# Two tiles of v loaded in five transfers each: 112 rows, then two sets of eight rows

## The chip, the core and the metric

The kernel runs on one core of one Trainium2 chip. It is written in Bass, with the Tile framework for buffers and semaphores; the order of the work on each engine is the order of the program (`manual_schedule`). A core has a tensor engine (PE; its weight loads stand in the profile as PEld), a vector engine (DVE), a scalar engine (ACT), a general engine (POOL), a sequencer for transfers (SP), and 16 DMA engines that all queues share. The metric is the time of one execution on the device in microseconds. Before the change the median of three runs is 256.0 us (255.96 to 256.0).

## The reference

Two stages in a row. The first is a cross-covariance attention over channels, with q, k and v of shape 4 x 6400 x 256 in float32:

```
qn = q / (norm(q over the 6400 rows) + 1e-6);  kn likewise
a  = softmax(kn^T @ qn / tau)            # 256 x 256 for each of the 4 batches
x  = v @ a                               # 4 x 6400 x 256
```

The second is a mixture of eight rank-16 adapters on the 25600 rows of x: `logits = x @ w_gate`, the two largest of eight are chosen for each row and weighted by their softmax, and `out = x + sum over the chosen e of w_e * (x @ A_e) @ B_e`.

## The kernel before

A batch's 6400 rows lie on the 128 partitions as 128 x 50: partition p holds rows 50p to 50p + 49. One of the 50 is a chunk (128 rows of 256 channels). All loads of q, k and v are issued by POOL, and they turn float32 into bf16 on the way. A chunk is 1 KB of float32 for each partition, and 512 bytes in the tile.

The q and k of a batch come in five tiles of 10 chunks. The v of a batch comes in three tiles of 18, 16 and 16 chunks (`VP`), into a ring of three buffers (`VB`), and each tile of 18 takes one row of 18 KB from each partition's part of DRAM. Tile (b, s) is tile s of batch b. For the first batch each v tile is loaded in two transfers; for batches 1 and 2 each is one transfer of 128 rows; the very last tile has three.

Phase one works on batch 0 alone: for each chunk two matmuls add to the 256 x 256 product of k and q (`gram`, L217), ACT or DVE squares it (`square`, L207 and L209), and matmuls with ones sum the squares (`norm`, L228). A chain of small steps (`chain0` to `chain6`) turns this into the attention matrix. Then come 100 slots, 25 for each batch. A slot takes two chunks of v: four transposes on PE (L366), a copy out of PSUM, the product with the gate and the adapters (L472), and a slot or two later the product with the attention matrix (L488), the adapters' second product (L508) and a copy to a row of `ys` (L512). Five slots make a group; its output is one store of 1280 KB. The gram of the next batch is dealt into the same slots (`GRAM`), so that PE always has both.

The loads stand in one list, sorted by the slot at which each is needed; `load_more` walks down it, as far as buffers are free, at the start of every slot. So the loads go to POOL's queue in one fixed order. A buffer is free when its last reader is done; POOL then waits for that reader, and everything behind on POOL's queue waits with it. POOL does nothing else after the first 12 us. Stores of finished groups are held back (`send`, `DEFER`) and issued from ACT; the last ones go out from SP in smaller parts (`LAST`).

Completion of a transfer is counted by a semaphore that each of the 16 DMA engines raises by one when its share has landed; a waiting engine waits for all 16. The loads take eight such semaphores in turn, and the trace shows POOL waiting for the load eight before the one it is about to issue: the load that is issued at 68.87 us takes the semaphore of the load that landed at 68.34 us, the next, at 71.31 us, that of 70.76 us.

The change touches `load_more` (L151 is the load of a v tile) and adds a function beside it.

Of the kernel before, what the change touches and what calls it, by code (L numbers as in the profile page):

```python
# [16 lines left out]
def kernel(  # L17
# [16 lines left out]
    nc = tc.nc  # L34
    B, N, C = q.shape
    P = 128
# [13 lines left out]
    VP = [18, 16, 16]  # L50
    FIRST = 4
    DEFER = 7

    GRAM = {1: (0, 20), 2: (24, 45), 3: (49, 67)}
    assert B == 4 and NC == 50
# [3 lines left out]
    v_v = v.rearrange("b (p c) d -> b p c d", p=P)  # L59
# [24 lines left out]
    for b, (first, last) in GRAM.items():  # L84
        n = last - first + 1
        for c in range(NC):
            s = first + c * n // NC
# [28 lines left out]
    def piece(kind, c):  # L116

        if kind == "qk":
            return divmod(c, PC)
        s = 0  # L120
        while c >= VP[s]:
            c -= VP[s]
            s += 1
        return s, c

    def used(kind, b, c, n):
        left[kind][where[kind, b, piece(kind, c)[0]]] -= n

    def load_more(limit=1000):

        while limit and at_load[0] < len(loads):
            _, kind, b, s, o, parts = loads[at_load[0]]
            if (kind, b, s) not in where:
                n = len(left[kind])
                if n >= bufs[kind] and left[kind][n - bufs[kind]]:
                    return
                where[kind, b, s] = n
                left[kind].append(PC if kind == "qk" else VP[s])
                if kind == "qk":
                    t = qk_pool.tile([P, 2, PC, C], BF16, tag="qk", name="qk")  # L140
                else:
                    t = v_pool.tile([P, max(VP), C], BF16, tag="v", name="vt")
                tiles[kind][b, s] = t
            t = tiles[kind][b, s]
            c0 = s * PC if kind == "qk" else sum(VP[:s])
            for m in parts:
                if kind == "qk":
                    nc.gpsimd.dma_start(t[:, 0, o:o + m, :], q_v[b, :, c0 + o:c0 + o + m, :])  # L148
                    nc.gpsimd.dma_start(t[:, 1, o:o + m, :], k_v[b, :, c0 + o:c0 + o + m, :])
                else:  # L150
                    nc.gpsimd.dma_start(t[:, o:o + m, :], v_v[b, :, c0 + o:c0 + o + m, :])  # L151
                o += m
            at_load[0] += 1
            limit -= 1
# [11 lines left out]
    nc.sync.dma_start(bst, moe_B.rearrange("e r d -> (e r) d"))  # L166
    nc.sync.dma_start(ast, moe_A.rearrange("e (p cc) r -> p e (cc r)", p=P))
    load_more(3)
    ones_bf = const.tile([P, P], BF16)
    nc.vector.memset(ones_bf, 1.0)  # L170
# [4 lines left out]
    for c in range(0, FIRST, 2):  # L175
        t = tiles["qk"][0, 0]
        nc.vector.tensor_copy(t[:, 0, c:c + 2, :], stage[:, 0, c:c + 2, :])
        nc.scalar.copy(t[:, 1, c:c + 2, :], stage[:, 1, c:c + 2, :])
    load_more(1)
    ident = const.tile([P, P], BF16)  # L180
    make_identity(nc, ident)
    ident_f = const.tile([P, P], FP32)
    make_identity(nc, ident_f)
    load_more(3)

    wg_sb = const.tile([P, CC, E], BF16)
# [335 lines left out]
    def send(keep):  # L522


        eng = nc.scalar
        while len(unsent) > keep:
            gr = unsent.pop(0)
            c0, n = 2 * (gr["f"] - gr["b"] * NPAIR), 2 * gr["n"]
            eng.dma_start(out_v[gr["b"], :, c0:c0 + n, :], gr["ys"][:, 0:n, :])
# [43 lines left out]
    while nz < NPT or zq is not None or dq is not None:  # L573
# [26 lines left out]
        dq, zq = zq, u  # L600
        send(max(0, min(DEFER, DEFER - (slot - GRAM[B - 1][1]) // 4)))
        if behind:
# [53 lines left out]
```

## Time and profile before

The profiled execution took 255.87 us, of which the page's span is 254.1 us; 1.8 us lie around it. The median of the three runs, 256.0 us, is 0.1 us above it.

| what | value |
|---|---|
| median of 3 runs | 256.0 us |
| profiled execution, its span | 255.87 us, 254.1 us |
| PE busy | 220.4 us (87%) |
| ACT busy | 176.1 us (69%) |
| DVE busy | 152.7 us (60%) |
| POOL busy | 33.0 us (13%) |
| mean granted TensorE clock | 0.966 |
| HBM read, written | 78.91 MB, 26.21 MB: 414 GB/s over the span |

A row of the page's table of groups is: line, engine, operation, what it writes and reads, count, busy time and mean length. The page's second part cuts the span in 40 slices; its row DMA gives in tenths how busy the 16 DMA engines were together. The third part lists the queues: q0 is POOL's loads, q10 is ACT's stores, q1 is SP's transfers, q8 and q14 carry the engines' instructions. The sixth part lists transfers by issuing line, with the median time from issue to landing. The chain of work that ended last is followed back from the last instruction, and each step stands for what released the next one.

### The profile page before, as it was taken

The page shows a single profiled execution, that of the slowest core. Times are in us where ns is not written, and L with a number is a line of the kernel's source. Part 1 is how long each engine was busy: PE and PEld are TensorE (multiplying, and loading weights), DVE is VectorE, ACT ScalarE, POOL GpSimd, SP SyncE. Part 2 cuts the span into 40 slices and gives each one's busy share as a digit, 9 for nine tenths or more (in the row PEclk, how much of TensorE's full clock was granted, in tenths as well). Part 3 has the DMA queues.
Part 4 walks back from the last instruction along what each step waited for, and adds up shares of the span by engine and source line. Part 5 has one row for each costly group of instructions (what it writes and reads, how often), then busy time and mean ns, then how long its engine had stood idle before and what let it go on. Part 6 is the DMA issues. An engine that isn't in the chain of part 4 may idle for free.

```text
span 254.1 us, 7393 instructions
## 1 busy us (share of the span) xinstructions
PE 220.4 (87%) x3106; PEld 190.2 (75%) x3106; DVE 152.7 (60%) x577; ACT 176.1 (69%) x290; POOL 33.0 (13%) x67
## 2 busy tenths in 40 slices
PE   0787793985999999999999989999999899999950
PEld 0444461775899978989999778989997799998940
DVE  1322235453567678685776876767587876778720
ACT  3434344776488698887878778888867777887860
POOL 8131221112112100110110202000000200000000
PEclk9999998696899999999999999999999999999997
DMA  7999999999999999999999999999999999999995
GB/s 213 223 217 215 212 216 214 213 216 216 210 214 215 223 207 215 218 212 214 215 220 211 214 270 259 236 296 281 255 291 292 389 326 362 414 420 426 423 412 220
DMA packets 13745, 66.80 MB, mean 263 GB/s; under 512 B 2576, under 2 KB 2704, under 8 KB 10384
## 3 DMA queue, kind: packets, MB, share of 16 engines
q0 software_dynamic: 8496, 38.80, 74.8%
q10 hardware_dynamic: 2592, 23.59, 22.4%
q1 hardware_dynamic: 2624, 3.94, 4.7%
q8 instruction: 24, 0.39, 0.6%
q14 instruction: 9, 0.07, 0.1%
HBM read 78.91 MB, written 26.21 MB: 414 GB/s over the span
## 4 chain that ended last, share of the span: by engine, by line
PE 58%; DMA 25%; DVE 7%; ACT 3%; issue 2%; POOL 1%; DVEq 0%; POOLq 0%; ACTq 0%
DMA qk<-in_k_dram 20%; PE y_ps L488 15%; PE acc L217 11%; PE zg L472 7%; PE y_ps L508 7%; PE vT_ps L366 6%; DMA out_dram<-ys 5%; PE zg L496 4%; PE nrm L234 3%; PE vT_ps L387 3%; ACT sq L207 2%; DVE gz L476 2%; ACT ys L512 1%; DVE lm L422 1%; DVE e L418 1%
## 5 line engine op out<-in xcount | busy, mean ns | idle before, releaser
L207 ACT ACTIVATE sq<-qk 128x1024 bf16<-128x1024 bf16 x87 | 89.6, 1054 | 22.1 <-DMA qk<-in_k_dram 16.8
L217 PE MATMUL acc<-qk 128*128 128x256 bf16 x400 | 74.7, 287 | 15.3 <-DMA qk<-in_k_dram 8.8
L512 ACT COPY ys<-y_ps 128x512 f32<-128x512 f32 x100 | 58.8, 588 | 22.9 <-PE y_ps L508 19.7
L488 PE MATMUL y_ps<-a_bf,vT 128*128 128x256 bf16 x400 | 60.3, 273 | 0.3 <-ACT ys L512 0.3
L217 PEld LDWEIGHTS <-qk 128*128 128x128 bf16 x400 | 34.4, 102 | 25.4 <-DMA qk<-in_k_dram 11.8
L476 DVE TENSOR_TENSOR gz<-zg,gate 128x256 bf16<-128x256 f32 x100 | 41.7, 418 | 14.7 <-PE zg L472 13.4
L377 DVE COPY vT<-vT_ps 128x512 bf16<-128x512 bf16 x63 | 26.7, 424 | 28.2 <-PE vT_ps L366 27.6
L234 PEld LDWEIGHTS <-sq 128*128 128x128 bf16 x600 | 36.3, 98 | 7.2 <-ACT sq L207 3.1
L366 PE MATMUL vT_ps<-ident,vt 128*128 128x128 bf16 x400 | 39.5, 223 | 0.9 <-DMA vt<-in_v_dram 0.7
L472 PE MATMUL zg<-wa_sb,vT 128*128 128x128 bf16 x400 | 38.7, 220 | 1.2 <-DVE gzT L502 1.0
L508 PE MATMUL y_ps<-ball_sb,gzT 128*128 128x256 bf16 x200 | 38.2, 273 | 0.0
L234 PE MATMUL nrm<-ones_bf,sq 128*128 128x1 bf16 x600 | 35.9, 165 | 1.2 <-ACT sq L207 1.2
L488 PEld LDWEIGHTS <-vT 128*128 128x128 bf16 x400 | 33.6, 97 | 3.2 <-issue 0.4
L366 PEld LDWEIGHTS <-vt 128*128 128x128 bf16 x400 | 30.2, 99 | 3.4 <-DMA vt<-in_v_dram 0.8
L496 PE MATMUL zg<-ident,gz 128*128 128x128 bf16 x200 | 27.9, 222 | 1.1 <-DVE gz L476 0.6
L375 ACT COPY vT<-vT_ps 128x512 bf16<-128x512 bf16 x37 | 21.7, 587 | 10.3 <-PE vT_ps L366 8.9
L472 PEld LDWEIGHTS <-vT 128*128 128x128 bf16 x400 | 26.1, 97 | 3.4 <-issue 2.2
L502 DVE COPY gzT<-zg 128x256 bf16<-128x256 bf16 x90 | 25.3, 281 | 0.0
L148 POOL DMA_DIRECT2D qk<-in_q_dram x21 | 11.4, 545 | 91.1 <-ACT sq L207 23.6
L209 DVE TENSOR_TENSOR sq<-qk 128x1024 bf16<-128x1024 bf16 x13 | 9.0, 693 | 22.3 <-DMA qk<-in_k_dram 15.4
L496 PEld LDWEIGHTS <-gz 128*128 128x128 bf16 x200 | 15.3, 99 | 2.9 <-DVE gz L476 2.5
L151 POOL DMA_DIRECT2D vt<-in_v_dram x17 | 9.0, 534 | 64.4 <-PE y_ps L508 45.5
(61 smaller groups left out, 183.6 us busy)
## 6 DMA issues: line engine op xcount, KB each, us to landing
out_dram<-ys ACTq DMA_DIRECT2D x18, 1280.0 KB, 13.1
qk<-in_q_dram POOLq DMA_DIRECT2D x18, 640.0 KB, 20.9
qk<-in_k_dram POOLq DMA_DIRECT2D x18, 640.0 KB, 23.1
vt<-in_v_dram POOLq DMA_DIRECT2D x5, 1024.0 KB, 26.9
vt<-in_v_dram POOLq DMA_DIRECT2D x3, 1152.0 KB, 25.3
vt<-in_v_dram POOLq DMA_DIRECT2D x6, 512.0 KB, 22.1
out_dram<-ys SPq DMA_DIRECT2D x3, 512.0 KB, 8.7
out_dram<-ys SPq DMA_DIRECT2D x4, 256.0 KB, 7.6
```

Of the source, the lines that this page charges most:

```text
L207: nc.scalar.activation(sq, src, ACT.Square)
L217: nc.tensor.matmul(acc[b][:, ic, :], t[:, 1, o, ic * P:(ic + 1) * P], t[:, 0, o, :], start=(c == 0 and ic == 0), stop=(c == NC - 1), skip_ ...
L234: nc.tensor.matmul(nrm[b][:, j:j + 1], sq[:, w, c % 2, ic * P:(ic + 1) * P], ones_bf[:, 0:1], start=(c == 0 and j == 0), stop=(c == NC - 1 ...
L366: nc.tensor.matmul(pt[:, ic, sc * P:(sc + 1) * P], vt[:, o + sc, ic * P:(ic + 1) * P], ident, is_transpose=True, start=(i == 0), stop=(i = ...
L377: nc.vector.tensor_copy(dst, src)
L472: nc.tensor.matmul(z[:, sc, :], r["vT"][:, ic, sc, :], st[b]["wa"][:, ic, E:E + ER], start=(sc == 0 and ic == 0), stop=(sc == 1 and ic == ...
L476: nc.vector.tensor_tensor(out=gz.rearrange("p c (e r) -> p c e r", e=E), in0=z.rearrange("p c (e r) -> p c e r", e=E), in1=gr["gate"][:, r ...
L488: nc.tensor.matmul(y[:, sc, :], r["vT"][:, ic, sc, :], st[b]["a"][:, ic, :], start=(sc == 0 and ic == 0), stop=False, skip_group_check=True)
L496: nc.tensor.matmul(gt[:, sc, :], r["gz"][:, sc, :], ident, is_transpose=True, start=(sc == 0), stop=(sc == 1))
L502: nc.vector.tensor_copy(gzT, gt)
L508: nc.tensor.matmul(r["y"][:, sc, :], r["gzT"][:, sc, :], ball_sb, start=False, stop=(sc == 1), skip_group_check=True)
L512: nc.scalar.copy(gr["ys"][:, r["w"]:r["w"] + 2, :], r["y"])
```

## The change

Two loads are issued otherwise: the 18-chunk tile of batch 1 and that of batch 2, which were one transfer of 128 rows of 18 chunks each. Each becomes five transfers, all still on POOL's queue and in the same place of the order: rows 0 to 111 with all 18 chunks; then of the rows 112, 114, ..., 126 the first 17 chunks, and then the 18th chunk; then the same two for the rows 113, 115, ..., 127. The four small ones carry a limit on the longest piece, `max_dma_last_dim`, of 512 bytes a chunk: 8704 and 512 bytes, half the float32 bytes of a row. The same bytes move to the same places. Nothing else changes.

```diff
+    LEANED = [(1, 0), (2, 0)]
...
+    def leaned_load(t, src, n):
+        nc.gpsimd.dma_start(t[0:112, 0:n, :], src[0:112, :, :])
+        for j in range(2):
+            for c0, c1 in ((0, n - 1), (n - 1, n)):
+                nc.gpsimd.dma_start(t[112 + j:P:2, c0:c1, :], src[112 + j:P:2, c0:c1, :],
+                                    max_dma_last_dim=(c1 - c0) * C * 2)
...
+            if kind == "v" and (b, s) in LEANED:
+                leaned_load(t, v_v[b, :, c0:c0 + parts[0], :], parts[0])
+                parts = []
```

## The prediction

> **What bounds the kernel now.** I read the slices first, then the queues, then one window from the middle, then the chain. In the slices the row DMA is what to look at.
>
> ```profile
> PE   0787793985999999999999989999999899999950
> DMA  7999999999999999999999999999999999999995
> ...
> q0 software_dynamic: 8496, 38.80, 74.8%
> q10 hardware_dynamic: 2592, 23.59, 22.4%
> q1 hardware_dynamic: 2624, 3.94, 4.7%
> q8 instruction: 24, 0.39, 0.6%
> q14 instruction: 9, 0.07, 0.1%
> ```
>
> The 16 DMA engines are at nine tenths or more from the second slice to the last but one; their packets sum to 102.6% of the span (neighbouring packets overlap by 0.019 us). PE is nearly as full from slice 13 on. In the window from 60 to 150 us the load queue alone fills the engines:
>
> ```profile
> DMA packets 3907, 19.42 MB, mean 216 GB/s; under 512 B 433, under 2 KB 433, under 8 KB 3363
> q0 software_dynamic: 3875, 19.04, 103.4%
> q8 instruction: 11, 0.18, 0.7%
> vt<-in_v_dram POOLq DMA_DIRECT2D x2, 1152.0 KB, 24.9
> ```
>
> The last row holds the two transfers that change. They lie behind others for 25 us: the queue is deep, and only how long the engines work counts.
>
> The chain then shows where transfers hold up the rest, and where it stops:
>
> ```profile
> 181.41 13.06 DMA out_dram<-ys
> 194.47 0.02 issue
> 194.49 0.02 ACTq L512
> 194.51 0.04 issue
> 194.55 0.59 ACT ys L512
> ...
> 245.25 0.23 PE y_ps L508 x2
> 245.49 0.02 issue
> 245.51 0.58 ACT ys L512
> ```
>
> At 194 us ACT waits for a store's landing before it may refill a row of `ys`. The last computation ends at 246.1 us, but the span ends at 254.1 us: the rest is stores still in the engines.
>
> So the slowest engine ends the span, and the engines are not equal. The trace's completion records give, for each transfer, when each of its 16 shares landed. Behind the first share, in us:
>
> ```
> load issued at 16.41 (34.34): 0 0 0 .1 .1 .2 .2 .2 .2 .3 .3 .3 .3 .4 .5 1.5
> load landing from 111.69:  0 .04 .24 .30 .43 .47 .59 | 1.09 1.15 1.19 1.30 1.32 1.37 1.41 1.48 1.57
> last store (249.36):       0 .1 .2 .2 .3 | 1.0 | 2.6 2.8 | 3.3 3.3 3.4 3.5 3.6 3.6 3.7 3.7
> ```
>
> At 31 us all lie within 0.48. Each of the 24 packets of q8 (16 KB, 0.89 to 0.98 us) puts one engine 1.1 us further back and it never makes that up (0.36 to 1.48 after the packet at 32.0, still 1.48 at 112 us). Their lengths repeat with period eight (936, 975, 974, 961, 893, 893, 951, 945 ns, then 935, 975, 974, 961...) and the second round hits engines that the first had hit: eight engines take three each. These are the eight at 3.3 to 3.7 at the end. The nine packets of q14 (0.31 to 0.32 us) fall on three others, most on one (0.15 to 0.66 to 1.19 to 1.73), which is then at 2.3 to 2.8; one more drifts back between 221 and 245 us by 0.3 a store, with no packet that explains it. Five are ahead by over 3 us.
>
> **The change part by part.** Prices first, from starts of neighbouring packets on one engine: a row of 4 chunks 0.154 us, 10 chunks 0.380, 16 chunks 0.605, 18 chunks 0.681. That is 0.0376 a chunk and 0.003 a packet. A completion packet is 0.022.
>
> Removed, for each tile: one 128-row transfer, eight 18-chunk rows an engine: 8 x 0.681 = 5.45 us.
>
> Added on every engine: 112 rows are seven an engine, 4.77 us, and four completions more, 0.09 us. Then 16 rows of 17 chunks and 16 of one. The trace before has no transfer of eight rows. A set of eight can feed eight engines at most; both long sets may fall on the same eight, or on all 16. The first is my base, because the one-chunk transfers between them are as many rows as a long set and would take the other eight in turn; the second is a rival.
>
> An engine with two long rows has 2 x 0.643 more (by the line above; between 0.605 and 0.681, the rows of 16 and 18 chunks; cut in two pieces it is 0.003 dearer), in all 4.77 + 0.09 + 1.29 = 6.14 us, +0.69 (0.61 to 0.77). An engine with two short rows has 2 x 0.041 (up to 0.154, the 4-chunk row, the nearest one measured; I take the line, which fits all four rows): 4.94, -0.51 (-0.51 to -0.29). Two tiles: **+1.4 (1.2 to 1.5) on eight engines, -1.0 (-1.0 to -0.6) on the other eight.** Mean 0.2 more, the completions.
>
> Semaphores and POOL: POOL issues eight more transfers at 0.53 us (L151), 4.2 us of an engine that is 13% busy. More matters that it waits for the load eight before. For tile (1,0) the first part goes at 68.87 us as now, the others as the loads that landed at 70.76, 73.82, 76.94 and 79.37 release them, and the q load that now goes at 71.31 goes after the landing at 81.79, at about 82.1; its k at 85.1. Their data have their turn at 93.4 and 96.4, so ten us of queue still cover them and no engine runs dry. For tile (2,0) the q load moves from 122.01 to about 129 and its turn is 140: covered too. Without that cover it would cost 7 to 11 us, once a tile.
>
> PE waits for up to four more semaphores at the first transpose of a tile (0.05 us each by the one such wait of L366): 0.4 us at most, and PE has cover: on the engine that lands first the last store took 3.2 us from issue at 246.12, on the slowest 6.9. PE may be 3.7 us late before it sets the end. The same covers the wait at 194 us, where a lag is felt about 1.6-fold (4.6 for the 2.9 that the packets make), since stores and loads take turns: 2.2 us later at worst. Tile (1,0) lands at 93.42 and is first read at 95.10, tile (2,0) at 140.3 for 147.5: 0.7 and 1.4 later still does.
>
> What is late next: the last store is over when its slowest engine is. That decides on which eight the long rows fall, and no record before the change gives the engines' numbers.
> If among them are fetching engines (the eight hit by q8), 3.3 to 3.7 becomes 4.7 to 5.1: +1.0 to +1.4. With all eight the figure is +1.4, and 255.87 + 1.4 = **257.3 us**.
>
> The Trainium skill, page "DMA: Bandwidth & Descriptors", section on why a DMA increments its semaphore by 16, says that a load issued from GpSimd over fewer than 16 engines takes consecutive ones from a round-robin cursor; by that the two long sets fall on the same eight, which agrees with the base, and the trace before cannot show it. The same page's section "Anatomy of one DMA" charges each such transfer a fixed 2.0 us; by that eight more would be 16 us. Against it stand two loads of four chunks that land 1.25 us apart (32.74 and 33.99), which is eight rows of 0.154 and one completion, with nothing left for a fixed part.
>
> **The rivals.**
> First, the light share falls on just the eight fetching engines. They end at 2.3 to 2.7. But the two others that are late, at 2.6 and 2.8, get the long rows: 4.0 and 4.2, +0.5, 256.4 us. For it speaks that the fetching engines are eight, as many as a set. Against a gain speaks the count: ten engines are late at the end and only eight can be made lighter.
> Second, on the other side, the same but the two late ones do not hold: the one that drifts does so for no reason that the records show, and if a more loaded engine does not drift, and the other's packets of q14 fall where it has slack, the end is set at 2.7 and the kernel gains 1.0: 255.0 us (wait at 194 us shorter too). It decides as soon as both end under 2.3 before the change's 1.4.
> Third, long rows spread evenly: every engine has 0.2 us more, 256.1 us; the change does then not do what it is shaped for.
> Fourth, the small transfers each stall the queue. Four-chunk loads show no such stall; at 0.5 us each it would be 4 us, 260 us.
>
> **How the numbers follow.** Long rows on fetching engines: 0.52 (nearly all of it all eight, 257.3; own range 256.8 to 258.1, the upper end with long rows at 0.681 and PE's waits showing). Light on the eight with the two late ones holding: 0.24, 256.4. The same with a gain: 0.15, 255.0. Even: 0.06. Stalls: 0.03. A measurement tells about 0.2%, 0.5 us, from no change. Slower: 0.48 of the first, 0.05 of the second, 0.03 of the last: 0.56. Faster: 0.15 and 0.03 from the second case: 0.18. The same: 0.26. The range leaves out half of the gains and the stalls: 255.2 to 258.1.
>
> **What would show it.** The loads row of 1152 KB drops from three to one, with rows of 1008, 68 and 4 KB beside it. In the completion records the 16 shares of the loads after 94 us should split by 1.2, and after 141 us by 2.4, eight against eight. If the fetching ones are the long ones, the last store's spread grows from 3.7 to about 5 us and the last computation still ends near 246 us; if not, the spread falls to 2.7 to 4. An unchanged spread shows even rows. Wrong would be the whole account if the last computation itself moved by the 1.4 us or if a slice of the row DMA fell under nine before 245 us.

## The result and the profile after

The changed kernel takes **256.89 us** (median of seven runs, 256.82 to 257.77), the kernel before on the same chip 256.0 us (median of seven, 255.96 to 256.34): a ratio of **1.0037, 95% interval 1.0025 to 1.0048**. It is slower by 0.9 us (0.4%). The profiled execution took 256.89 us with a span of 255.1 us, against 255.87 and 254.1 before: 1.02 us more. The granted TensorE clock was 0.962 (0.966 before).

The transfers of the changed kernel, from the slices, the queues and the list of issues (columns of the last: count, KB each, median us from issue to landing):

```profile
DMA  7999999999999999999999999999999999999994
...
q0 software_dynamic: 8848, 38.80, 74.8%
q10 hardware_dynamic: 2592, 23.59, 22.3%
...
vt<-in_v_dram POOLq DMA_DIRECT2D x2, 1008.0 KB, 25.5
...
vt<-in_v_dram POOLq DMA_DIRECT2D x1, 1152.0 KB, 26.8
...
vt<-in_v_dram POOLq DMA_DIRECT2D x4, 68.0 KB, 21.6
...
vt<-in_v_dram POOLq DMA_DIRECT2D x4, 4.0 KB, 18.4
```

The bytes are the same, the packets of the load queue 352 more, and the engines stay at nine tenths to the last slice but one. No slice shows a hole. The starts and lengths of the packets say it more sharply: a packet starts 0.019 us before the end of the one ahead of it on its engine (behind a completion packet, at its end), so the packets of an engine can be strung together. In the kernel before, none of the 16 engines pauses for over 0.03 us between 60 us and its last packet. With the change there are three pauses, 0.14 us at 194.6 us on one of the late engines, 1.06 at 199.9 and 0.29 at 200.7. The two longer ones begin as the first two engines are done with the store issued at 195.80 us, so they lie on the two that are furthest ahead.

The waits between 100 and 200 us (engine and line that waited, what ended the wait; us in total, times, longest). Line L380 is the transposes, L526 the copy to `ys`:

```profile
ACT ys L526 <- DMA out_dram<-ys: 1.9, 1, 1.9
...
PEld L380 <- DMA vt<-in_v_dram: 1.4, 1, 1.4
...
PE vT_ps L380 <- DMA vt<-in_v_dram: 1.2, 1, 1.2
```

The wait of ACT for a store was there before, in this line:

```profile
ACT ys L512 <- DMA out_dram<-ys: 1.7, 1, 1.7
```

TensorE's wait for a load of v was not. The chain of work that ended last goes through both (start, length, what):

```profile
142.47 28.05 DMA vt<-in_v_dram
...
182.25 13.30 DMA out_dram<-ys
...
195.63 0.59 ACT ys L526
...
246.59 0.58 ACT ys L526
```

The first line is tile (2,1), the tile behind the second changed one. It landed at 168.28 us before and lands at 170.51 now; its first reader had wanted it at 169.73. TensorE, which stood 0.5 us earlier than before until then, stands 0.84 us later from here on. So the store of 181.41 is issued at 182.25; it lands at 195.55 instead of 194.47, and from ACT's wait for it to the last computation (246.1 before, 247.2 now) everything is 1.08 us later.

The completion records show the shares split. The 16 shares behind the first, in us:

```
before, load landing in full at 96.44: 0 .02 .17 .23 .27 .29 .41 .47 .57 .66 1.10 1.16 1.24 1.38 1.46 1.51
after, load landing in full at 96.89:  0 .02 .18 .18 .79 .79 .97 1.01 1.01 1.08 1.33 1.43 1.54 1.63 | 1.94 2.01
before, last store, shares from 249.36 to 253.04: 0 .1 .2 .2 .3 | 1.0 | 2.6 2.8 | 3.3 3.3 3.4 3.5 3.6 3.6 3.7 3.7
after, last store, shares from 250.57 to 254.07:  0 .0 .1 .5 .6 | 1.2 1.2 1.3 1.4 1.4 1.6 1.9 | 2.9 3.0 3.4 3.5
```

Fitted to the first pair, the difference between an engine with long rows and one with short rows comes out at 1.14 to 1.20 us, an estimate. Ten engines were late at the end before; now four are. The latest is still the one that counts, and it is 1.03 us later. The spread itself has not grown, since the last store is issued 1.08 us later and so its first share lands 1.21 us later.

Which of the eight fetching engines got long rows can be read in part. Six packets of q8 (the instruction queue) have fallen by 94 us. An engine with both a fetch and long rows then stands near 2 us behind the first, and there are two such, at 1.94 and 2.01. The packets at 112.9 and 122.0 us strike just these: in the load that lands in full at 129.13 us they stand at 3.05 and 3.12. The two fetching engines that the first six packets left out are struck at 98.4 and 105.6 us, when their shares are at 0.05 and 0.0: they have short rows. So the long rows fell on **two of the eight**.

### The profile page after: what moved, and what is told of

Its sections match the earlier page's. It is cut to its first block, busy times and chain, and to the rows that moved or that the text cites. A ratio compares the mean times of both kernels' runs of the same rounds, so it can differ in the third digit from the quotient of the medians.

```text
span 255.1 us, 7405 instructions
## 1 busy us (share of the span) xinstructions
PE 219.9 (86%) x3106; PEld 189.9 (74%) x3106; DVE 152.6 (60%) x577; ACT 176.1 (69%) x290; POOL 37.2 (15%) x75
## 4 chain that ended last, share of the span: by engine, by line
PE 50%; DMA 36%; DVE 6%; ACT 2%; issue 2%; POOL 1%; DVEq 0%; ACTq 0%; POOLq 0%
DMA qk<-in_k_dram 20%; PE y_ps L502 13%; DMA vt<-in_v_dram 11%; PE acc L231 9%; PE zg L486 6%; PE y_ps L522 6%; PE vT_ps L380 6%; DMA out_dram<-ys 5%; PE zg L510 4%; PE vT_ps L401 3%; PE nrm L248 3%; DVE gz L490 1%; ACT sq L221 1%; PE nrm L242 1%; DVE lm L436 1%
## 5 line engine op out<-in xcount | busy, mean ns | idle before, releaser
L526 ACT COPY ys<-y_ps 128x512 f32<-128x512 f32 x100 | 58.7, 587 | 24.3 <-PE y_ps L522 21.0
L380 PE MATMUL vT_ps<-ident,vt 128*128 128x128 bf16 x400 | 39.4, 222 | 1.9 <-DMA vt<-in_v_dram 1.7
L380 PEld LDWEIGHTS <-vt 128*128 128x128 bf16 x400 | 29.9, 99 | 4.5 <-DMA vt<-in_v_dram 2.1
L165 POOL DMA_DIRECT2D vt<-in_v_dram x15 | 8.0, 536 | 58.5 <-PE y_ps L522 44.4
```

What stands on the lines that cost most here:

```text
L380: nc.tensor.matmul(pt[:, ic, sc * P:(sc + 1) * P], vt[:, o + sc, ic * P:(ic + 1) * P], ident, is_transpose=True, start=(i == 0), stop=(i = ...
L526: nc.scalar.copy(gr["ys"][:, r["w"]:r["w"] + 2, :], r["y"])
```

## The experiments

The first round asked whether the cost comes from unequal rows or from eight more transfers. All times below are medians; each comparison is with runs of the kernel before on the same chip (256.01 us for this round, 17 runs). The short form below calls the set of eight rows with even numbers, chunks 1 to 17, L0 and its 18th chunk S0; L1 and S1 are those with odd numbers. The change is 112 rows, L0, S0, L1, S1. In the edits, which are shown in part, `part(j, r0, r1, c0, c1)` loads the rows r0 to r1 - 1 of set j (0 even, 1 odd) with the chunks c0 to c1 - 1; n is 18 and m is 17 unless the edit says otherwise.

**Long sets on the other eight engines** (112 rows, S0, L0, S1, L1):

```diff
+        part(0, 0, 8, m, n)
+        part(0, 0, 8, 0, m)
+        part(1, 0, 8, m, n)
+        part(1, 0, 8, 0, m)
```

> The same five transfers a tile, but of each set the one-chunk transfer goes first and the 17-chunk one second. Theory U (unequal rows: the four small transfers fall on eight engines each in turn, and the end is that of the latest engine): the long rows now fall on the other eight engines. By the completion records of the changed kernel six of the eight fetching engines were short and two long; now six are long. The last store's latest share is again a fetching engine with long rows, 3.3 to 3.7 + 1.4 behind the first share of before: +1.0 to +1.4 us against before (256.9 to 257.4 us), and in the last store six shares instead of two stand near the end. Theory T (the price is that of eight more transfers, wherever their rows fall): the same time as the changed kernel, 256.9, with the same number of late shares.

258.21 us (257.49 to 258.26), ratio 1.0076 (1.0064 to 1.0088). The same bytes, packets and transfers, turned by eight engines, cost more than twice as much as the change: 2.2 us, more than either expectation allowed. Behind the first changed tile four shares stand at 2.56 to 2.69, and the packets at 97.7 and 105.4 us strike engines at 1.75 and 1.61, too far behind for short rows alone: six of the eight fetching engines have long rows, the complement of the change's two. Tile (2,1) lands at 171.20, and the last store ends 2.4 us later than before.

**Even rows** (112 rows, L0, L1, S0, S1):

```diff
+        part(0, 0, 8, 0, m)
+        part(1, 0, 8, 0, m)
+        part(0, 0, 8, m, n)
+        part(1, 0, 8, m, n)
```

> The same five transfers a tile in another order: the two 17-chunk ones one after the other, then the two of one chunk. Theory U: the long sets fall on different halves, each engine has one long and one short row, and only the completions remain: +0.1 to +0.2 us against before (256.1 to 256.2), and the shares of the last store are spread as before, 3.7 us with the same ten late ones. Theory T: as many transfers, rows and bytes as the changed kernel, so its time, +0.9 us.

256.18 us (256.0 to 256.53, 11 runs), ratio 1.0006 (0.9997 to 1.0015), in the expectation by unequal rows. Behind the first changed tile the shares reach from 0 to 1.74 us without a split of 1.2 (0 to 1.56 ahead of it). The load queue carries the change's packets, and TensorE waits for tile (2,1) as it does with the change:

```profile
q0 software_dynamic: 8848, 38.80, 74.9%
...
PEld L385 <- DMA vt<-in_v_dram: 1.3, 1, 1.3
```

(queue: packets, MB, share of the engines; wait: total, times, longest). TensorE stood 1.1 us earlier than before until then, and 0.1 us later after the wait. The last computation ends 0.73 us later than before, the last share of the last store 0.34 us later.

Eight transfers more, with every extra issue and completion, cost 0.2 us or nothing. This settles it against the price of the transfers: **the unequal rows make the change slower**.

**Turned by two and by six engines**, by two or six of the short rows issued ahead of L0, the rest last:

```diff
+        part(0, 0, 2, m, n)
+        part(0, 0, 8, 0, m)
+        part(1, 0, 8, m, n)
+        part(1, 0, 8, 0, m)
+        part(0, 2, 8, m, n)
```

That is the turn by two; the turn by six has a 6 in place of each 2.

> The first one-chunk transfer is cut in two, of two rows and of six; the two rows go first, the six last, so that, if engines are taken in turn, both long sets move on by two engines. Theory U: two outcomes, by where the fetching engines lie. If the long eight then hold no fetching engine: the fetching ones end 1.0 earlier, the two other late ones 1.4 later at 4.0 and 4.2, +0.3 to +0.5 us (256.3 to 256.5). If they hold four: +1.0 to +1.4 with four shares near the end. Theory T: one transfer more a tile than the changed kernel, +1.0 us, nothing moved in the shares.

> As the one before, but six rows go first and two last: the long sets move on by six engines. Theory U: eight or four of the fetching engines are long (eight if they lie six behind the first long one, four if they lie two ahead): +1.0 to +1.5 us, with eight or four shares near the end; spread of the last store 4.5 to 5.2. Theory T: +1.0 us, nothing moved in the shares.

By two: 257.08 us (257.0 to 257.23), ratio 1.0041 (1.0029 to 1.0053). By six: 258.14 us (257.51 to 259.3), ratio 1.0089 (1.0066 to 1.0111). Behind the first tile three shares stand at 2.30 to 2.50 in the first, five at 2.28 to 2.91 in the second, where the packet at 99.0 us strikes one more engine with long rows. So three and six fetching engines have long rows, where the expectations had none, four or eight; the 2.1 us of the turn by six are above the 1.0 to 1.5 that were expected. Time follows that count: 0 (even rows) 1.0006, two 1.0037, three 1.0041, six 1.0076 and 1.0089; two and three can't be told apart.

The second round (256.16 us before, 21 runs) asked for a turn that spares the fetching engines, and where the cost sits.

**Turned by fourteen**, with long rows of 16 chunks and the 17th and 18th as sets of short rows, eight transfers a tile:

```diff
+        m = n - 2
+        part(0, 0, 8, m, m + 1)
+        part(1, 0, 6, m, m + 1)
+        part(0, 0, 8, 0, m)
+        part(0, 0, 8, m + 1, n)
+        part(1, 0, 8, 0, m)
+        part(1, 6, 8, m, m + 1)
+        part(1, 0, 8, m + 1, n)
```

> Both tiles, with the long rows (now 16 chunks, the chunks 17 and 18 as two sets of short rows) turned by fourteen engines against the change, by fourteen short rows issued ahead of the first long set. Theory U (what counts is how many of the eight fetching engines get long rows: two in the change, four when turned by two, eight when turned by six, six when turned by eight): turned by fourteen it is none. The fetching engines get 2 us of work less, the other eight 2.8 us more; those of the others that were already late (two of the ten late shares in the last store of the kernel before) then set the end. Load of tile (2,1) lands between 168.0 and 169.8 us (168.28 before, 170.51 with the change), no wait of TensorE of over 0.8 us for it, 255.5 to 256.7 us in all. Rival P (it is the order that costs: short pieces issued ahead of long ones keep the long ones back and bunch them, on whatever engines they fall): the most short rows stand ahead of a long set here, fourteen, so it is at least as slow as when turned by six or eight, 258.1 us or more, and tile (2,1) lands after 171.2 us.

On tile (1,0) alone (`LEANED = [(1, 0)]`):

> The same turn by fourteen on the first of the two tiles alone. Theory U: the fetching engines get 1 us less, the others 1.4 us more, of which only one or two were late; 255.4 to 256.3 us, load of tile (2,1) between 167.8 and 169.0 us. Rival P: half of what the turn by six or eight costs on two tiles, 257.0 to 257.2 us.

264.99 us (264.56 to 265.89), ratio 1.0357 (1.0342 to 1.0372), and 260.47 us (260.24 to 261.0), ratio 1.0171 (1.0157 to 1.0185): worse than either theory allowed, for a reason that neither named. POOL issues the next load only at 94.05 us in the first kernel and 93.71 in the second, when the first of the tile's eight transfers has landed, and the row DMA has a hole there:

```profile
DMA  7999999999999969999997999999999999999995
```

That is the first kernel, with a second, smaller one behind its second tile. Nothing could be read on the engines from these two.

**The change on one tile**, (1,0) alone:

```diff
-    LEANED = [(1, 0), (2, 0)]
+    LEANED = [(1, 0)]
```

> The change on tile (1,0) alone. Theory U: two fetching engines are 0.7 us later instead of 1.4 us, so the load of tile (2,1) lands near 169.4 us (half of the 2.23 us by which the change puts it back), after its first reader wants it at 169.7 us less the half microsecond that TensorE is early; TensorE waits some 0.3 us or less for it, and the run takes 256.1 to 256.6 us. If both tiles are needed for a stall, 256.0 us; if the cost sits on the first tile alone, 256.9 us.

256.40 us (256.11 to 256.55, 11 runs), ratio 1.0008 (0.9999 to 1.0016). Tile (2,1) lands at 170.05, later than the half that was expected, and TensorE waits 0.9 us for it; but the run is only 0.24 us longer. The time is within the expectation. TensorE had stood 0.65 us earlier than before until the wait and stands 0.37 us later behind it, so the length of a wait alone does not tell what it costs.

**The change on a late tile**, (3,0) alone:

```diff
-    LEANED = [(1, 0), (2, 0)]
+    LEANED = [(3, 0)]
```

> The change on tile (3,0) alone, which is loaded from 168.6 us on and lands at 193.9 us, behind the load of tile (2,1) at which TensorE waits with the change. If that wait and the store it delays are the path (theory U as it now stands), TensorE's groups up to 190 us stand where they stood before within 0.3 us, tile (2,1) lands within 0.5 us of 168.3 us, and what is left is 0.7 us more on two fetching engines for the stores behind it: 256.0 to 256.5 us. If instead the extra bytes on two late engines at the end of the program set the time by themselves, as the prediction had it, the last share is 0.7 us later and the run takes 256.6 to 256.8 us.

256.56 us (256.29 to 256.66, 11 runs), ratio 1.0015 (1.0006 to 1.0024). Tile (2,1) lands at 169.00 (0.7 later than before, outside the half microsecond), TensorE has no wait for it, the last store is issued 0.23 us later than before, and its last share lands 0.70 us later, at 253.74. In time it is 0.40 us, between the two ranges that were expected; the 0.7 us of the last share are what the second one said. This speaks for the engines' own work at the end, and against the wait at tile (2,1) as the only path.

The third round (256.13 us before, 21 runs) repeated the turn by fourteen with fewer transfers and separated the hole.

**Turned by fourteen in six transfers**, on tile (1,0); the second long set has 16 chunks:

```diff
+            part(112, 126, 1, m, n)
+            part(112, 127, 2, 0, m)
+            part(113, 128, 2, m - 1, m)
+            part(113, 128, 2, 0, m - 1)
+            part(126, 128, 1, m, n)
```

Here `part` takes the first row, the end and the step of the rows, then the chunks: fourteen short rows, L0, eight rows of one chunk, L1 with 16 chunks, two short rows.

> The turn by fourteen on tile (1,0) once more, in six transfers instead of eight (112 rows; fourteen short rows; a long set of 17 chunks; eight rows of one chunk; a long set of 16 chunks; two short rows), so that three loads are still under way behind it when GpSimd waits for the tile. The run in eight transfers left the DMA engines empty from 94.4 to some 96 us, since the next load was issued only at 93.7 us, and so said nothing on the engines. Theory U (the eight fetching engines all get short rows): each of them has about half a microsecond less work, the other eight 0.7 us more; the late shares of the last store go from 3.69 to about 3.2 to 3.5 us, tile (2,1) lands between 167.8 and 169.3 us (168.28 before, 170.05 with the change on this tile alone, 256.4 us), and the run takes 255.5 to 256.1 us. Rival P (the order of short and long pieces costs, whatever the engines): not below the change on this tile alone, 256.4 us or more, tile (2,1) at 170 us or later. If the sixth transfer already empties the DMA queue, 258 us or more.

256.52 us (256.36 to 256.91, 11 runs), ratio 1.0018 (1.0009 to 1.0026). No gain, so the expectation by the engines failed, and the rival's ranges were met: 256.4 us or more, tile (2,1) at 170 us or later (170.47; the profiled execution is the slowest of the eleven). Two shares stand at 2.41 and 2.69 behind the tile, so again two fetching engines have long rows, the complement of the six of the turn by six. There is no hole in the row DMA. Among these orders the count can be turned from two to six and not to none.

**The same on both tiles**, the second in the order six short rows, L0, S1, L1, two short rows:

```diff
+            part(112, 123, 2, m, n)
+            part(112, 127, 2, 0, m)
+            part(113, 128, 2, m, n)
+            part(113, 128, 2, 0, m)
+            part(124, 128, 2, m, n)
```

> The same on both tiles, the second in the order six short rows, long set, eight short rows, long set, two short rows, which starts from the place to which the first tile has turned the engines, so that its long rows fall on the same eight. Theory U: fetching engines 1.0 us lighter, the others 1.4 us heavier; of these, one or two were late by 2.6 to 2.8 us at the end of the kernel before and are now late by 4.0 to 4.2 us: 255.7 to 256.8 us, tile (2,1) at 167.5 to 169.8 us. Rival P: at least the 257.1 us of the turn by two; tile (2,1) at 171 us.

257.23 us (257.03 to 257.74), ratio 1.0045 (1.0032 to 1.0058), above the expectation by the engines and in that of the rival (257.1 us or more), though tile (2,1) lands at 170.24 us and not at 171. The profile is telling for another question, what sets the end. The last computation starts where it did before (245.51 us then):

```profile
245.53 0.58 ACT ys L538
```

but the last store's shares reach from 249.60 to 254.41, a spread of 4.82 us where it was 3.69. The last computation ends where it did, and the kernel is 1.1 us longer: the late engines alone set the end.

**The turn by fourteen on tile (3,0) alone:**

```diff
-    LEANED = [(1, 0), (2, 0)]
+    LEANED = [(3, 0)]
```

The six transfers are those of tile (1,0) above.

> The turn by fourteen in six transfers on tile (3,0) alone, behind the load of tile (2,1). The change's own order on this tile took 256.56 us, and the last share of the last store was 0.7 us later. Theory U: here the fetching engines get the short rows, so the last share is some half a microsecond earlier than before instead, and TensorE is where it was: 255.4 to 256.0 us. Rival P: as slow as the change's order on this tile, 256.5 us or more.

256.42 us (256.36 to 256.67, 11 runs), ratio 1.0013 (1.0004 to 1.0022). No gain here either, and 0.1 us under the 256.5 us of the rival: the last share is at 253.65, 0.6 later than before.

**Even rows in eight transfers**, tile (1,0) alone:

```diff
+        part(0, 0, 4, 0, m)
+        part(0, 4, 8, 0, m)
+        part(1, 0, 8, 0, m)
+        part(0, 0, 4, m, n)
+        part(0, 4, 8, m, n)
+        part(1, 0, 4, m, n)
+        part(1, 4, 8, m, n)
```

> Tile (1,0) in eight transfers with even rows: 112 rows; the long pieces as two sets of four rows and one of eight; the short pieces as four sets of four. Every engine gets the same bytes as before. If the 260.5 us of the turn by fourteen on one tile in eight transfers were the wait for the queue's eight places (the next load issued at 93.7 us, the engines empty behind it) and not the engines that got the long rows, this takes about as long, 259.3 to 260.8 us, with a gap on the DMA engines near 95 us. If it was the uneven rows, 256.0 to 256.4 us.

260.58 us (260.01 to 261.03), ratio 1.0172 (1.0159 to 1.0186), as long as the uneven rows in eight transfers (1.0171). The windows (us, busy time of PE, PEld, DVE, ACT and POOL, the TensorE clock, the share of the 16 DMA engines, GB/s) of the change:

```profile
90.00:93.00 3.00, 2.96 (x32) 2.41 (x30) 2.17 (x10) 2.69 (x7) 0.00 (x0) 1.00 0.99 194
93.00:96.00 3.00, 2.63 (x55) 2.21 (x53) 1.66 (x5) 3.00 (x7) 1.93 (x4) 1.00 1.05 206
```

and of this kernel:

```profile
90.00:93.00 3.00, 2.90 (x30) 2.32 (x28) 1.99 (x9) 2.69 (x5) 0.00 (x0) 1.00 0.74 138
93.00:96.00 3.00, 2.73 (x60) 2.53 (x61) 1.60 (x7) 3.00 (x8) 2.23 (x5) 1.00 0.35 41
```

The eighth part goes at 88.21 us. The next load is issued at 93.77, after the landing of the 112 rows at 92.83, which frees the first of the eight semaphores. By then the queue is nearly empty: the engines lose (1.05 - 0.74) x 3 + (1.05 - 0.35) x 3 = 3.0 us against their full 1.05, and TensorE then waits for k:

```profile
PE acc L239 <- DMA qk<-in_k_dram: 2.9, 1, 2.9
```

Of the change's five transfers the last goes at 79.46, and the loads issued at 82.62, 85.04 and 88.78 us cover the same wait. With six, two loads do.

## Why the prediction was right

**The bound: right.** The engines are full to the end and the latest of them ends the span. The kernel before has no pause on any engine, and the change none of over 0.14 us on a late one. The kernel with both tiles turned by fourteen in six transfers shows it by itself: the last computation unmoved, the spread 4.82 us, the time up by 1.1 us.

**The size: the step held, its base did not.** The step said: if any fetching engines are among the long eight, +1.0 to +1.4 us. Measured: the last share 1.03 us later, the profiled time +1.02, the medians +0.89. Within it, the base "all eight of them" (+1.4, 257.3 us) was wrong: two of eight, by the shares. The late engines at 3.3 plus 1.4 are 4.7, which is 1.0 over the 3.7 of before: an estimate by which the lower end is what two engines give that were not the very last. In part the range was met by luck. The step does not ask how many fetching engines get long rows, and with the same sets on the other eight engines, six of them, the kernel takes 258.21 us, above the range. That the order of the change falls on two was not foreseen.

**The prices: right.** 16 long rows and 16 short ones a tile, each cut in two packets; neighbouring pieces of 4352 bytes start 0.323 us apart, so 0.646 a row against 0.643 in the sum. The pieces of 256 bytes start 0.022 us apart. So two long rows against two short ones are 4 x (0.323 - 0.022) = 1.2 us a tile, as in the sum. The eight small issues cost 0.56 us each (0.53 in the sum), and POOL's busy time went from 33.0 to 37.2 us.

**On which engines: the assumption on sets of eight held.** L0 and L1 share eight engines, S0 and S1 the others, and swapping them turns two fetching engines with long rows into six. The Trainium skill, page "DMA: Bandwidth & Descriptors", section on why a DMA increments its semaphore by 16, has a load from GpSimd over fewer than 16 engines take consecutive ones from a round-robin cursor; the pairs here (two and six by a turn of eight, two by fourteen and six by six) agree. The fixed 2.0 us for a transfer on that page of the Trainium skill, in "Anatomy of one DMA", isn't seen: with even rows eight more transfers took 0.2 us.

**POOL's wait for the load eight before: right, and a near miss.** It said 82.1 and 85.1 us for the two loads behind the tile; they went at 82.62 and 85.04, covered. Its price without cover, 7 to 11 us a tile, was too high: eight transfers on one tile cost 4.3 and 4.45 us, on both 8.8.

**TensorE's cover: wrong.** The step checked the landing of tiles (1,0) and (2,0), both in time, and not that of the next one. Tile (2,1) had 1.45 us to spare, the lag reached 2.23 there, and TensorE waited. So "the last computation still ends near 246 us" and "the spread grows to about 5" both failed: the computation ended 1.1 us later and the spread was 3.5. The prediction had named a moved computation as a sign that the whole account is wrong. Two things say that it isn't. The cost comes without a moved computation (both tiles turned by fourteen in six). And in the change the latest engines have no pause of over 0.14 us, so their end is the sum of their packets, wherever TensorE stands. The kernels where TensorE waits and little is lost (even rows, tile (1,0) alone) show less than they seem to: TensorE had been early there and stands only 0.1 and 0.4 us later behind the wait, against 0.84 with the change. In most kernels here the last computation and the last share are late together, and what TensorE's lateness would cost by itself, without late engines, no run shows.

**The rivals.** Even rows fell to the reading of the shares, and the kernel with even rows gave the 256.1 us that this rival named (256.18). The stall fell with the same kernel. The two with short rows on all fetching engines were not met: no uneven order tried gave fewer than two.

**What stays open.** Six fetching engines with long rows cost 2.1 to 2.2 us, though the sum allows no more than 1.4. Part of it is in the packets. The load and store packets of 2 KB and more, which are the same in number and size, took some 1.1 us longer an engine with the sets swapped and 0.9 us longer in the turn by six than with the change, mostly between 180 and 210 us. With the sets swapped the 640 load packets of 8192 bytes took 639 ns on the mean, against 626 with the change, and the 2304 store packets of 10240 bytes 399 against 394. The pauses add up to some 8.5 and 4.2 us over all engines, against 1.5. TensorE waited 2.2 and 2.3 us for tile (2,1) in both. Why the packets take longer there was not shown. And on one tile the turn by fourteen (two fetching engines with long rows) wasn't better than the change's own order (1.0018 and 1.0008), so among orders with the same count something else may matter too (the intervals overlap). The rival of the later expectations, that the order of long and short pieces costs whatever the engines, is not excluded: it gave the times of the turn by fourteen in six transfers better. Against it stands that this turn, on both tiles, costs half of what six or eight short rows ahead of the first long set do (1.0045; 1.0089 and 1.0076).

## What to carry to other kernels

Where all DMA engines are full, as here, a transfer that gives some of them more than others is paid at the latest engine, and the shares of one completion record show how late each is before anything is changed; a mean over the engines hides it. To move work off late engines, one must know which they are: split blind, none of the eleven kernels with uneven rows was faster. Splitting one load into as many parts as the queue has places in flight empties it, so count the loads that are left behind the split one.

## What was not expected of the hardware

Eight transfers of one tile, even and small, left the DMA engines without work for 3.0 us and cost 4.45 us; five, on each of two tiles and with even rows, cost 0.2 us or nothing. TensorE's place between 60 and 90 us differed by -1.4 to +1.0 us from kernel to kernel, and these differences do not order the times. And the lengths of the fetched packets, which repeat with period eight, seem to mark the engines. With the same six transfers of tile (1,0) the packet at 105.6 us struck one of the first three shares in one kernel, the one at 106.7 us a share at 1.47 in the other. They are 974 and 961 ns long, two different places of the period, so this is no sign that the long rows fell otherwise; both kernels have two fetching engines with long rows behind this tile (shares behind the first, of a load before the packet and of one after it):

```
tile (1,0) alone, before: 0 .03 .17 .87 1.05 1.08 1.09 1.31 1.34 1.36 1.40 1.41 1.42 2.11 2.36 2.59
                   after: 0 .16 .92 1.05 1.06 1.14 1.20 1.30 1.36 1.38 1.40 1.42 1.47 2.14 2.38 2.64
both tiles,       before: 0 .26 1.08 1.14 1.27 1.33 1.40 1.42 1.47 1.51 1.59 1.62 1.65 1.80 2.25 2.40
                   after: 0 .26 1.10 1.14 1.32 1.33 1.46 1.47 1.55 1.60 1.68 1.69 1.80 2.28 2.42 2.56
```
